# Dynamic convolution and two-way maxout: tap products in one instruction, first chunk ahead of the weights, three of six tap additions moved to an accumulating DMA

## The chip, the cores and the metric

The kernel runs on 1 core of one Trainium2 chip. The metric is the device time of the whole program in microseconds (us). The profile's span is a little shorter (491.3 us; the first three runs of the kernel before have the median 492.15 us). Runs come with a state, fast or slow; unless said otherwise fast runs are compared. A ratio below is the mean time of one kernel's fast runs over the mean of the other's fast runs in the same rounds, so it is not quite the ratio of the medians that are quoted.

## The reference, cut to what matters

For each of 8 x 4160 tokens, the softmax of 7 weights per head (8 heads) mixes the token's own row and the six rows before it; the result goes through a maxout layer:

```python
w = exp(weight_gen - max); w = w / sum(w)           # (B, S, 8, 7)
out = einsum('bshk,bskhg->bshg', w, x_unf)          # 7 taps, 192 channels
h1 = x @ w1;  h2 = x @ w2                           # 192 -> 1024, x is now `out`
y = maximum(h1, h2) @ w_out                         # 1024 -> 192
```

The kernel uses max(h1, h2) = h1 + relu(h2 - h1): it keeps w2 - w1 ("wd") for the hidden layer and folds w1 @ w_out into small matrices ("w10") once at the start.

## The kernel before

Each of the 128 partitions holds 260 token columns. A **chunk** of mostly 16 columns is loaded and convolved at a time; a **unit** of 8 columns is what TensorE takes per pass of the outer loop, so a chunk is mostly two units. At the ends both are smaller: chunks 0 to 2 give units 0 to 3, chunk 3 gives units 4 and 5, and so on. One chunk on VectorE (the `yield` lines and the address patterns are cut):

```python
def conv(ci):                                   # a generator, stepped between units
    sum_t = reduce_sum(e_t); rec_t = reciprocal(sum_t)   # e_t: the exponential, by ScalarE
    en_t = e_t * rec_t
    mul(0, 3)                                   # m_t[k] = x shifted by k * weight k, taps 0..2
    mul(3, 6)
    add(m_t[:, 0:3 * n], 0, 3, 3)               # taps 0..2 += taps 3..5
    mul(6, 7)
    add(m_t[:, 0:n], 0, 1, 1)
    add(m_t[:, 2 * n:3 * n], 2, 6, 1)
    add(y_t, 0, 2, 1)                           # y_t: the chunk's result
```

The outer loop, shortened:

```python
for u in range(NU + 1):
    target = UNITS[min(u + 3, NU - 1)][0]
    while queued <= target and queued < NCH:
        exp(queued)                             # ScalarE
        conv_q.append(queued); queued += 1
        load(loaded); loaded += 1               # GpSimd's DMA queue: weights and x of a later chunk
    if u + 1 < NU:
        conv_flush(UNITS[u + 1][0])             # the chunk that unit u + 1 needs, to its end
        transpose(u + 1)                        # DMA transpose y_t -> yt, from SyncE's queue
    for i in range(4):
        # hidden matmuls of unit u (hdp), ReLU on ScalarE (rd_t), output matmuls of unit u - 1 (op_ps)
        ...
        conv_step(1)
```

Each engine has its own list of instructions, in the order in which they are written here, and in the timelines shown below it works through it in that order: the exponential of chunk 5, at 117.15 us, stands behind the last ReLU of unit 4, at 116.23.

The softmax here doesn't subtract the row's maximum and nothing guards it: scores larger than these inputs give would overflow.

## Time and profile before

| | before |
|---|---|
| time, median | 492.15 us |
| TensorE busy | 426.4 us (87%) |
| VectorE busy | 421.4 us (86%) |
| a two-unit chunk on VectorE / on TensorE | 25.70 / 25.24 us |
| first hidden matmul / first of unit 4 | 47.19 / 102.64 us |
| x load of a big chunk, issue to landing | 8.0 us |
| transpose, issue to landing, median | 5.4 us |

The two engines are nearly balanced, so neither may get slower.

### The profile page before, as it was taken

Reading aid. Unit: us, or ns where it says so; the run is one execution under the profiler, and the core shown is the slowest. Engines: PE = TensorE matmul, PEld = TensorE weight load, DVE = VectorE, ACT = ScalarE, POOL = GpSimd, SP = SyncE. Lnnn points to the kernel's source line nnn. Section 1 sums busy time; section 2 is a strip of 40 time slices with the busy share of each in tenths; the row PEclk is TensorE's granted clock in tenths of the full one; section 3 lists DMA queues with packets and bytes.
Section 4 is the critical chain, followed back from the end, with each engine's and each line's share of the span. In section 5 each row is a group of like instructions: output and inputs, shape, how many; then the busy total and the mean of one; then the engine's idle time right before and its main releaser. Section 6 shows DMA issues by size and latency. Waiting matters only on the chain.

```text
span 491.3 us, 8185 instructions
## 1 busy us (share of the span) xinstructions
PE 426.4 (87%) x3598; PEld 270.3 (55%) x3598; DVE 421.4 (86%) x185; ACT 336.5 (68%) x436; POOL 20.6 (4%) x43
## 2 busy tenths in 40 slices
PE   0041958569999999999999999899999999999997
PEld 0030524336666666665666666566666666666676
DVE  0178999999999999999999999999999999996000
ACT  1142728438787878786787878687878787877774
POOL 2000000000000000000000000000000000000000
PEclk9995979869999999999999999999999999999999
DMA  7726475473929192919383848556474838062312
GB/s 181 242 66 117 87 168 136 77 178 58 261 42 267 33 242 64 248 65 215 105 213 106 176 145 138 182 126 195 96 224 78 232 58 209 1 192 66 114 66 97
DMA packets 62164, 68.36 MB, mean 139 GB/s; under 512 B 52313, under 2 KB 53593, under 8 KB 60336
## 3 DMA queue, kind: packets, MB, share of 16 engines
q1 hardware_dynamic: 58000, 42.30, 31.3%
q0 software_dynamic: 4128, 25.54, 24.6%
q8 instruction: 28, 0.46, 0.4%
q14 instruction: 8, 0.07, 0.0%
HBM read 47.56 MB, written 25.56 MB: 149 GB/s over the span
## 4 chain that ended last, share of the span: by engine, by line
PE 73%; DVE 13%; DMA 11%; issue 1%; ACT 1%; SPq 0%; POOL 0%; POOLq 0%; DVEq 0%
PE op_ps L310 31%; PE hdp L261 20%; PE hdp L276 12%; DMA yt<-y_t 7%; PE op_ps L297 6%; DVE m_t L140 6%; DVE m_t L149 4%; PE op_ps L305 4%; DMA ws<-in_moe_w_dram 2%; DMA wso<-in_moe_w_out_dram 1%; DVE en_t L128 1%; DVE y_t L149 1%; DMA xb_t<-in_x_dram 1%; DVE sum_t L122 1%; DVE rec_t L125 1%
## 5 line engine op out<-in xcount | busy, mean ns | idle before, releaser
L287 ACT ACTIVATE rd_t<-hdp 128x1024 bf16<-128x1024 f32 (+1 forms) x272 | 267.6, 986 | 115.0 <-PE hdp L276 77.1
L310 PE MATMUL op_ps<-wo,rd_t 128*128 128x192 bf16 x2080 | 215.4, 247 | 0.0
L310 PEld LDWEIGHTS <-rd_t 128*128 128x128 bf16 x2080 | 177.0, 98 | 23.5 <-issue 0.6
L140 DVE TENSOR_TENSOR m_t<-xb_t,en_t 128x9216 bf16<-128x9216 bf16 (+5 forms) x54 | 188.8, 3524 | 0.6
L149 DVE TENSOR_TENSOR m_t<-m_t 128x3072 bf16<-128x3072 bf16 (+5 forms) x54 | 136.8, 2561 | 0.6
L261 PE MATMUL hdp<-yt,wdE 128*128 128x512 bf16 (+1 forms) x272 | 101.9, 375 | 31.6 <-DMA yt<-y_t 30.2
L261 PE MATMUL hdp<-yt,wdO 128*128 128x512 bf16 (+1 forms) x272 | 102.0, 375 | 0.0
L276 PE MATMUL hdp<-yt,wdR 64*128 64x512 bf16 (+1 forms) x544 | 82.1, 378 | 1.0 <-ACT rd_t L287 1.0
L321 ACT COPY o_t<-op_ps 128x384 f32<-128x384 f32 x130 | 61.6, 474 | 2.5 <-PE op_ps L310 2.3
L276 PEld LDWEIGHTS <-wdR 64*128 64x128 bf16 x544 | 16.3, 94 | 58.7 <-issue 58.3
L261 PEld LDWEIGHTS <-wdE 128*128 128x128 bf16 x272 | 26.8, 98 | 34.9 <-DMA yt<-y_t 20.0
L297 PE MATMUL op_ps<-w10R,yt 128*128 128x384 bf16 x130 | 44.0, 339 | 0.0
L297 PEld LDWEIGHTS <-yt 128*128 128x128 bf16 x130 | 12.4, 96 | 53.2 <-issue 52.8
L128 DVE TENSOR_TENSOR en_t<-e_t,rec_t 128x1792 bf16<-128x1792 bf16 (+2 forms) x18 | 33.2, 1845 | 0.6
L305 PEld LDWEIGHTS <-yt 128*128 128x128 bf16 x260 | 25.6, 98 | 14.6 <-issue 0.3
L305 PE MATMUL op_ps<-w10E,yt 128*128 128x192 bf16 x130 | 32.2, 248 | 0.0
L305 PE MATMUL op_ps<-w10O,yt 128*128 128x192 bf16 x130 | 32.1, 247 | 0.0
L149 DVE TENSOR_TENSOR y_t<-m_t 128x3072 bf16<-128x3072 bf16 (+2 forms) x18 | 28.8, 1602 | 0.6
L261 PEld LDWEIGHTS <-wdO 128*128 128x128 bf16 x272 | 26.8, 98 | 2.6 <-issue 2.6
L214 PE MATMUL tp<-ident,w1E 128*128 128x128 bf16 x8 | 2.2, 274 | 25.1 <-ACT w1E L197 16.8
L102 POOL DMA_DIRECT2D xb_t<-in_x_dram x17 | 9.0, 530 | 350.3 <-DVE m_t L140 350.3
L122 DVE TENSOR_REDUCE sum_t<-e_t 128x128 f32<-128x896 bf16 (+2 forms) x18 | 17.8, 989 | 4.4 <-ACT e_t L112 4.4
(30 smaller groups left out, 67.4 us busy)
## 6 DMA issues: line engine op xcount, KB each, us to landing
out_dram<-o_t SPq DMA_DIRECT2D x31, 768.0 KB, 3.5
xb_t<-in_x_dram POOLq DMA_DIRECT2D x14, 1056.0 KB, 8.0
wg_t<-in_weight_gen_dram POOLq DMA_DIRECT2D x14, 448.0 KB, 8.9
ws<-in_moe_w_dram SPq DMA_DIRECT2D x4, 512.0 KB, 8.8
xb_t<-in_x_dram POOLq DMA_DIRECT2D x2, 672.0 KB, 8.6
ws<-in_moe_w_dram SPq DMA_DIRECT2D x4, 256.0 KB, 10.8
xb_t<-in_x_dram POOLq DMA_DIRECT2D x1, 864.0 KB, 7.3
wso<-in_moe_w_out_dram SPq DMA_DIRECT2D x1, 768.0 KB, 6.4
```

Source lines behind the costliest of these rows:

```text
L102: nc.gpsimd.dma_start(out=xb_t, in_=bass.AP(tensor=x.tensor, offset=(c0 - PAD) * D, ap=[[CPP * D, P], [1, (To + PAD) * D]]),)
L122: nc.vector.reduce_sum(out=sum_t, in_=_sub(e_t, 0, [[K, TH], [1, K]]), axis=AX.X)
L128: nc.vector.tensor_tensor(out=_sub(en_t, 0, [[2, TH], [2 * TH, K], [1, 2]]), in0=_sub(e_t, 0, [[K, TH], [1, K], [0, 2]]), in1=_sub(rec_t, ...
L140: nc.vector.tensor_tensor(out=m_t[:, k0 * n:k1 * n], in0=_sub(xb_t, k0 * D, [[D, nk], [1, n]]), in1=_sub(en_t, k0 * TH * 2, [[2 * TH, nk], ...
L149: nc.vector.tensor_tensor(out=dst, in0=m_t[:, a * n:(a + w) * n], in1=m_t[:, b * n:(b + w) * n], op=ALU.add)
L261: nc.tensor.matmul(hd_ts[u, f][:, j * 512:j * 512 + N], lhsT=wd[kind][:, f * P:(f + 1) * P], rhs=_sub(yt_ts[u], 2 * j * P, [[3 * P, n // 2 ...
L276: nc.tensor.matmul(hd_ts[u, f][:, j * 512:j * 512 + N], lhsT=wd["R"][r, f * P:(f + 1) * P], rhs=_sub(yt_ts[u][r, :], P, [[3 * P, n // 2], ...
L287: nc.scalar.activation(out=_sub(rd_ts[u], f * 1024, [[512, 2], [1, N]]), in_=_sub(hd_ts.pop((u, f)), 0, [[512, 2], [1, N]]), func=AF.Relu,)
L297: nc.tensor.matmul(op[:, 0:2 * D], lhsT=yt[:, (3 * i + 1) * P:(3 * i + 2) * P], rhs=w10R, start=True, stop=False, skip_group_check=True,)
L305: nc.tensor.matmul(op[:, sl], lhsT=yt[:, (3 * i + 2 * j) * P:(3 * i + 2 * j + 1) * P], rhs=(w10E, w10O)[j], start=False, stop=False, skip_ ...
L310: nc.tensor.matmul(op[:, sl], lhsT=rd[:, f, j * 512 + i * P:j * 512 + (i + 1) * P], rhs=wo[:, f * D:(f + 1) * D], start=False, stop=(f == ...
L321: nc.scalar.copy(out=o_ts[u][:, 2 * i * D:2 * (i + 1) * D], in_=op_ts.pop((u, i))[:, 0:2 * D])
```

## The change

The intent is to free VectorE. The seven products become one instruction. Three of the six additions (taps 0..2 += taps 3..5) go to a DMA that adds to its destination. As that takes a while, the remaining additions of a chunk (`conv2`) are issued one chunk later, behind the products of the next chunk. Chunk 0 is also loaded and convolved before the weights are prepared, and the weights are loaded only once. The core of the diff, with cuts:

```diff
-        mul(0, 3) ... mul(3, 6) ... add(m_t[:, 0:3 * n], 0, 3, 3) ... mul(6, 7) ... (further adds)
+        nc.vector.tensor_tensor(out=m_t, in0=_sub(xb_t, 0, [[D, K], [1, n]]), in1=..., op=ALU.mult)
+        if ci + 2 < len(CHUNKS):
+            load(ci + 2)
+        m_ts[ci] = m_t
+        nc.gpsimd.dma_start(out=m_t[:, 0:3 * n], in_=m_t[:, 3 * n:6 * n], accum_op=ALU.add,
+                            max_dma_last_dim=4096)
+
+    def conv2(ci):
+        nc.vector.tensor_tensor(out=rows(m_t, 2, 2, 0), in0=rows(m_t, 2, 2, 0),
+                                in1=rows(m_t, 5, 2, 1), op=ALU.add)
+        nc.vector.tensor_tensor(out=y_t, in0=m_t[:, 0:n], in1=m_t[:, 2 * n:3 * n], op=ALU.add)
...
+        exp(0); conv(0); conv2(0)              # ahead of the weight differences
...
     for u in range(NU + 1):
+        while queued < NCH and queued <= UNITS[min(u + 3, NU - 1)][0]:
+            exp(queued)
+            conv(queued)
+            if queued > 1:
+                conv2(queued - 1)
+            queued += 1
         if u + 1 < NU:
-            conv_flush(UNITS[u + 1][0])
             transpose(u + 1)
```

More of the change, by code (lines that the diff above doesn't have):

```diff
@@ L51 @@
         c += 16
-    CHUNKS.append((c, [8, CPP - c - 8] if CPP - c > 8 else [CPP - c]))
+    while c < CPP:
+        CHUNKS.append((c, [min(8, CPP - c)]))
+        c += 8
     assert sum(sum(u) for _, u in CHUNKS) == CPP
@@ L67 @@
     psm = ctx.enter_context(tc.tile_pool(name="psm", bufs=1))
+    pm = ctx.enter_context(tc.tile_pool(name="pm", bufs=2))
     pen = ctx.enter_context(tc.tile_pool(name="pen", bufs=2))
@@ L73 @@
     wg_ts, xb_ts, y_ts, yt_ts = {}, {}, {}, {}
-    e_ts = {}
+    e_ts, m_ts = {}, {}
     zero_t = consts.tile([P, PAD * D], BF16, name="zero_t")
@@ L122, in conv @@
         nc.vector.reduce_sum(out=sum_t, in_=_sub(e_t, 0, [[K, TH], [1, K]]), axis=AX.X)
-        yield
         rec_t = psm.tile([P, TH], FP32, name="rec_t", tag="rec")
@@ L133, in conv, with rows @@
         )
-        yield
         xb_t = xb_ts.pop(ci)
-        m_t = psm.tile([P, K * n], BF16, name="m_t", tag="m")
-        def mul(k0, k1):
-            nk = k1 - k0
-            nc.vector.tensor_tensor(
-                out=m_t[:, k0 * n:k1 * n],
-                in0=_sub(xb_t, k0 * D, [[D, nk], [1, n]]),
-                in1=_sub(en_t, k0 * TH * 2,
-                         [[2 * TH, nk], [2, TH], [0, D // H // 2], [1, 2]]),
-                op=ALU.mult,
-            )
-        def add(dst, a, b, w):
-            nc.vector.tensor_tensor(out=dst, in0=m_t[:, a * n:(a + w) * n],
-                                    in1=m_t[:, b * n:(b + w) * n], op=ALU.add)
-        mul(0, 3)
-        yield
-        mul(3, 6)
-        yield
-        add(m_t[:, 0:3 * n], 0, 3, 3)
-        yield
-        mul(6, 7)
-        add(m_t[:, 0:n], 0, 1, 1)
-        yield
-        add(m_t[:, 2 * n:3 * n], 2, 6, 1)
+        m_t = pm.tile([P, K * n], BF16, name="m_t", tag="m")
+        nc.vector.tensor_tensor(
+            out=m_t,
+            in0=_sub(xb_t, 0, [[D, K], [1, n]]),
+            in1=_sub(en_t, 0, [[2 * TH, K], [2, TH], [0, D // H // 2], [1, 2]]),
+            op=ALU.mult,
+        )
+        if ci + 2 < len(CHUNKS):
[4 more added lines that the diff above has]
+    def conv2(ci):
+        n = sum(CHUNKS[ci][1]) * D
+        m_t = m_ts.pop(ci)
+        def rows(t, step, cnt, at):
+            return _sub(t, at * n, [[step * n, cnt], [1, n]])
+        nc.vector.tensor_tensor(out=rows(m_t, 2, 2, 0), in0=rows(m_t, 2, 2, 0),
+                                in1=rows(m_t, 5, 2, 1), op=ALU.add)
         y_t = py.tile([P, n], BF16, name="y_t", tag="y")
-        add(y_t, 0, 2, 1)
+        nc.vector.tensor_tensor(out=y_t, in0=m_t[:, 0:n], in1=m_t[:, 2 * n:3 * n], op=ALU.add)
         y_ts[ci] = y_t
-        yield
-    N_CONV = 6
+    load(0)
     ident = consts.tile([P, P], BF16, name="ident")
     make_identity(nc, ident)
-    load(0)
+    load(1)
     wd = {k: consts.tile([P, F], BF16, name="wd" + k) for k in "EOR"}
-    w1 = {k: consts.tile([P, F], BF16, name="w1" + k) for k in "ER"}
     wo = consts.tile([P, FCH * D], BF16, name="wo")
@@ L179 @@
     w10R = consts.tile([P, 2 * D], BF16, name="w10R")
-    def rows(kind):
-        return {"E": [(0, 0, P)], "O": [(0, 64, P)], "R": [(0, P, 64), (64, 0, 64)]}[kind]
-    with tc.tile_pool(name="pstage", bufs=2) as pstage, \
+    with tc.tile_pool(name="pstage", bufs=1) as pstage, \
          tc.tile_pool(name="pstage_ps", bufs=2, space=bass.MemoryType.PSUM) as pstage_ps:
-        for kind in "ERO":
-            st = []
+        ws = {}
+        for kind, r0, nr in (("E", 0, P), ("T", P, 64)):
             for wi, wsrc in enumerate((moe_w1, moe_w2)):
-                t = pstage.tile([P, F], FP32, name=f"ws{wi}", tag=f"ws{wi}")
-                for (p0, r0, nr) in rows(kind):
-                    nc.sync.dma_start(
-                        out=t[p0:p0 + nr, :],
-                        in_=bass.AP(tensor=wsrc.tensor, offset=r0 * F, ap=[[F, nr], [1, F]]),
-                    )
-                st.append(t)
-            if kind in w1:
-                nc.scalar.copy(out=w1[kind], in_=st[0])
-            nc.vector.tensor_tensor(out=wd[kind], in0=st[1], in1=st[0], op=ALU.subtract)
-        wso = pstage.tile([P, FCH * D], FP32, name="wso", tag="wso", bufs=1)
+                t = pstage.tile([nr, F], FP32, name=f"ws{wi}{kind}")
+                nc.sync.dma_start(
+                    out=t, in_=bass.AP(tensor=wsrc.tensor, offset=r0 * F, ap=[[F, nr], [1, F]]),
+                )
+                ws[kind, wi] = t
+        wso = pstage.tile([P, FCH * D], FP32, name="wso")
         nc.sync.dma_start(
@@ L203 @@
         )
-        nc.scalar.copy(out=wo, in_=wso)
-        exp(0)
-        for _ in conv(0):
-            pass
-        load(1)
-        w1t = pstage.tile([P, FCH * 2 * P], BF16, name="w1t", tag="w1t", bufs=1)
+        exp(0)
+        conv(0)
+        conv2(0)
+        for kind, dst in (("E", wd["E"]), ("T", wd["R"][0:64, :])):
+            nc.vector.tensor_tensor(out=dst, in0=ws[kind, 1], in1=ws[kind, 0], op=ALU.subtract)
+        nc.sync.dma_start(out=wd["R"][64:P, :], in_=wd["E"][0:64, :])
+        nc.sync.dma_start(out=wd["O"][0:64, :], in_=wd["E"][64:P, :])
+        nc.sync.dma_start(out=wd["O"][64:P, :], in_=wd["R"][0:64, :])
+        w1 = {}
+        for kind, nr in (("E", P), ("T", 64)):
+            w1[kind] = pstage.tile([nr, F], BF16, name="w1" + kind)
+            nc.scalar.copy(out=w1[kind], in_=ws[kind, 0])
+        nc.scalar.copy(out=wo, in_=wso)
+        w1t = pstage.tile([P, FCH * D], BF16, name="w1t")
         for fi in range(FCH):
-            tp = pstage_ps.tile([P, 2 * P], BF16, name="tp", tag="tp")
-            for j, kind in enumerate("ER"):
+            tp = pstage_ps.tile([P, D], BF16, name="tp", tag="tp")
+            for c0, kind, nr in ((0, "E", P), (P, "T", 64)):
                 nc.tensor.matmul(
-                    tp[:, j * P:(j + 1) * P], lhsT=w1[kind][:, fi * P:(fi + 1) * P],
-                    rhs=ident, is_transpose=True, skip_group_check=True,
-                )
-            nc.scalar.copy(out=w1t[:, fi * 2 * P:(fi + 1) * 2 * P], in_=tp)
-        nc.vector.memset(w10R, 0.0)
-        for d0, kind in ((0, "E"), (64, "O"), (P, "R")):
+                    tp[:, c0:c0 + nr], lhsT=w1[kind][:, fi * P:(fi + 1) * P],
+                    rhs=ident[0:nr, 0:nr], is_transpose=True, skip_group_check=True,
+                )
+            nc.scalar.copy(out=w1t[:, fi * D:(fi + 1) * D], in_=tp)
+        nc.gpsimd.memset(w10R, 0.0)
+        for p0, d0, nr, dst in ((0, 0, P, w10E), (0, 64, P, w10O),
+                                (0, P, 64, w10R[0:64, 0:D]), (64, 0, 64, w10R[64:P, D:2 * D])):
             pw = pstage_ps.tile([P, D], FP32, name="pw", tag="pw")
@@ L223 @@
                 nc.tensor.matmul(
-                    pw, lhsT=w1t[:, fi * 2 * P + d0:fi * 2 * P + d0 + P],
+                    pw[p0:p0 + nr, :], lhsT=w1t[:, fi * D + d0:fi * D + d0 + nr],
                     rhs=wo[:, fi * D:(fi + 1) * D],
@@ L227 @@
                 )
-            if kind == "E":
-                nc.scalar.copy(out=w10E, in_=pw)
-            elif kind == "O":
-                nc.scalar.copy(out=w10O, in_=pw)
-            else:
-                nc.scalar.copy(out=w10R[0:64, 0:D], in_=pw[0:64, :])
-                nc.scalar.copy(out=w10R[64:P, D:2 * D], in_=pw[64:P, :])
+            nc.scalar.copy(out=dst, in_=pw[p0:p0 + nr, :])
     prd = ctx.enter_context(tc.tile_pool(name="prd", bufs=2))
@@ L334 @@
     NCH = len(CHUNKS)
-    conv_q = []
-    conv_gen = {}
-    first_unit = [next(u for u in range(NU) if UNITS[u][0] == ci) for ci in range(NCH)]
-    def conv_step(k):
-        while k > 0 and conv_q:
-            ci = conv_q[0]
-            if ci not in conv_gen:
-                conv_gen[ci] = conv(ci)
-            try:
-                next(conv_gen[ci])
-                k -= 1
-            except StopIteration:
-                conv_q.pop(0)
-    def conv_flush(ci):
-        while ci not in y_ts:
-            conv_step(1)
-    transpose(0)
-    exp(1)
-    load(2)
-    conv_q.append(1)
-    conv_flush(1)
-    conv_step(1)
-    loaded, exped, queued = 3, 2, 2
+    queued = 1
     prev_evac = None
     for u in range(NU + 1):
-        target = UNITS[min(u + 3, NU - 1)][0]
-        while queued <= target and queued < NCH:
-            if exped <= queued:
-                exp(queued)
-                exped += 1
-            conv_q.append(queued)
+        while queued < NCH and queued <= UNITS[min(u + 3, NU - 1)][0]:
[3 more added lines that the diff above has]
+                conv2(queued - 1)
             queued += 1
-            if loaded < NCH:
-                load(loaded)
-                loaded += 1
+            if queued == NCH:
+                conv2(NCH - 1)
+        if u == 0:
+            transpose(0)
         if u + 1 < NU:
-            conv_flush(UNITS[u + 1][0])
             transpose(u + 1)
@@ L399 @@
                 prev_evac = (u - 1, q)
-            conv_step(1)
     if prev_evac is not None:
```

## The prediction

> **What bounds the kernel now.** I read the page top down: busy shares, slices, the chain that ended last, then instruction timelines and waits around two unit boundaries. A unit is the block of 8 (at the ends 4) token columns that TensorE handles in one pass of the outer loop. A chunk is what VectorE and one load handle, mostly two units.
>
> ```profile
> PE 426.4 (87%) x3598; PEld 270.3 (55%) x3598; DVE 421.4 (86%) x185; ACT 336.5 (68%) x436; POOL 20.6 (4%) x43
> ...
> PE   0041958569999999999999999899999999999997
> ...
> DVE  0178999999999999999999999999999999996000
> ...
> PE 73%; DVE 13%; DMA 11%; issue 1%; ACT 1%; SPq 0%; POOL 0%; POOLq 0%; DVEq 0%
> ```
>
> Two engines are nearly full. From slice 9 both rows are at 9, so this is a balance, not one bottleneck. The chain stays mostly on TensorE; its VectorE share sits in the first 97 us. Measured in the timeline: the result tiles (y_t) of successive big chunks end every 25.70 us (120.83, 146.52, 172.22), so VectorE's period is 25.70 us. Undisturbed, the first output matmul of a quarter unit recurs every 3.155 us, so a unit takes 12.62 us of TensorE and a two-unit chunk 25.24. VectorE is the slower by 0.46 us a chunk. After 102.64 the excess over the 3.155 us spacing adds up to only about 5 us. Relieving VectorE can therefore save 5 us there; the rest of the gain must come before 102.64.
>
> Three lines show how ScalarE ties VectorE to TensorE, in the timeline:
>
> ```profile
> 116.23 1.02 ACT L287 ACTIVATE rd_t<-hdp 128x1024 bf16<-128x1024 f32 x1 [0.26 <-PE hdp L261]
> 117.15 0.94 ACT L112 ACTIVATE e_t<-wg_t 128x896 bf16<-128x896 f32 x1
> ...
> 122.50 1.08 DVE L122 TENSOR_REDUCE sum_t<-e_t 128x128 f32<-128x896 bf16 x1
> ```
>
> The first is the last ReLU of unit 4, the second the exponential of chunk 5, which begins only when that ReLU is through. Its reader is the sum of chunk 5 at 122.50, when VectorE has finished chunk 4. It was ready 4.4 us early, so this tie costs nothing today.
>
> Three more show what a late y_t costs:
>
> ```profile
> 95.13 1.76 DVE L149 TENSOR_TENSOR y_t<-m_t 128x3072 bf16<-128x3072 bf16 x1
> 96.96 5.10 SPq L245 DMA_TRANSPOSE yt<-y_t  x2
> 102.64 0.61 PE L261 MATMUL hdp<-yt,wdE 128*128 128x512 bf16 x1 [9.45 <-DMA yt<-y_t]
> ```
>
> From the end of y_t (96.89) to the first matmul of its unit it is 5.75 us.
>
> **What the Trainium skill says.** "VectorE: DVE Perf Modes", section "The perf-mode tier table", gives bf16 tensor_tensor twice the base rate, 1224 ns for 2048 elements. The trace agrees: 9216 elements took 4955 ns and 3072 took 1751, hence 0.5215 ns an element plus 149 ns.
>
> "TensorE: Matmul & The Clock Gate", Part 1, says that an idle TensorE drops to half rate and recovers after about 3.4 us of work. The trace agrees; in the stretches around the stall of 9.45 us the granted clock (next to last but two) reads
>
> ```profile
> 100.00:105.00 5.00, 2.36 (x8) 0.52 (x9) 4.96 (x2) 0.68 (x1) 0.00 (x0) 0.50 1.04 185
> 105.00:110.00 5.00, 5.00 (x43) 3.56 (x42) 5.00 (x2) 3.21 (x6) 0.00 (x0) 0.91 0.41 161
> 110.00:115.00 5.00, 5.00 (x44) 2.94 (x42) 4.97 (x2) 3.78 (x5) 0.00 (x0) 1.00 0.00 0
> ```
>
> The unit that began at 102.64 lasted until about 116.77 (the next first output matmul, 117.83, less the usual 1.06), 14.13 us, so such a restart costs 1.5 us.
>
> "DMA: Bandwidth & Descriptors", section "SWDGE vs HWDGE vs iDMA", allows accumulation only from GpSimd's queue; so the additions share a queue with the x loads. "Collectives: The Full Stack", section "The bandwidth ceiling", says that an adding transfer reads two sources and so runs at half of about 31 GB/s per engine. The kernel before has none to compare.
>
> **The change part by part.**
>
> *VectorE per big chunk.* Before: three products (4955 + 4955 + 1752), additions 4958 + 2 x 1751, last addition 1758, and the softmax part, together 25.70 us. After, by the fit: one product of 21504 elements, 11.36; one addition over 6144, 3.35; the last, 1.76; the softmax part 4.16 (sum start to product start, 96.81 to 100.97). Sum 20.6 with gaps, 5 us less. VectorE's instructions are no longer the limit.
>
> *The accumulating DMA.* Source and destination of 3 x 3072 bf16 on 128 partitions are 2.36 MB each. Estimated from the Collectives page: 2.36 MB / (16 x 15.5 GB/s) = 9.5 us, behind an x load of 8.0 us (median to landing). DMA is busy 0.58 of the stretch 103 to 460, 14.9 us a chunk; with this 24.4.
>
> *The start.* The weights shrink from 3 to 1.5 MB and two row blocks come by copies. Chunk 0's product no longer waits for the weights: exponential at about 4.5, product at about 9.2 (its x lands as before, a little earlier), ending at 15. The accumulation follows the x load of chunk 2 and lands about 27; y_t at 30; weight differences 2.5; first hidden matmul at about 38 instead of 47.19. Then VectorE: products of chunks 1 and 2 until 49, a wait of about 5 for the accumulation, y_t of chunk 1 at 57, chunk 3's product until 73, y_t of chunk 2 at 75.6, chunk 4's product (its exponential comes after unit 2, about 76.5) until 93, y_t of chunk 3 at 98. Unit 4 starts at 98 + 5.75, about 104, against 102.64: the early start is eaten, because chunk 3's result now stands behind chunk 4's product.
>
> *The steady loop, which decides.* In the built order of the changed kernel, as of the one before, the exponential of chunk c+2 stands on ScalarE directly after the last ReLU of chunk c's first unit. On VectorE the final additions of chunk c+1 stand behind the product of chunk c+2, and the transpose of chunk c+1 waits for them. Before, that result stood ahead of chunk c+2's softmax. So now a closed loop exists, from a second unit's start to the next unit's start:
> - exponential begins 0.38 after it (117.15 against 116.77) and takes 0.94: 1.32
> - sum, reciprocal, weights: 4.16 plus 0.05 semaphore gap, to 5.53
> - product 11.36, to 16.9
> - two additions and gaps, 5.2, to 22.1
> - transpose and first matmul 5.75, to 27.8
>
> The unit that runs beside it takes 12.62, so TensorE stalls 15.2 us. Then comes the next first unit, restarting slow, 14.13. Period: 27.8 + 14.1 = 41.9 us instead of 25.70. Nothing in this loop is a full engine: VectorE works 20.6 of 41.9.
>
> Sum: unit 4 at 104; twelve periods bring unit 28 to 607. The chunk then pulled in has 8 columns: product 5.76 instead of 11.36, softmax 2.4 instead of 4.16, exponential 0.57 instead of 0.94, 7.8 less; unit 30 at 641. In the kernel before unit 30 started near 436.4 (first output matmul 437.50 less 1.06) and the end came 54.9 later; plus 1.5 for the slow restart: span 697. Time exceeds span by 0.85 (492.15 against 491.3): 698.
>
> **The rivals.**
> - *The loop is open and TensorE is the bound.* For it: VectorE falls to 20.6 against 25.24. Then 104 + (491.3 - 102.64 - 5), about 488. Against it: it needs the exponential ahead of the unit before, and the built order has it behind.
> - *DMA becomes the bound.* For it: 24.4 of 25.24 us, and slices where DMA is at 9 already. With an accumulation at 14 us the period is 29, some 540. Against it: the loop of 41.9 leaves it 17 us of slack, so it shows only if the loop is not there.
> - *A slow accumulation enters the loop.* The products of chunk c+1 end 41.9 us before its additions; load 8 plus accumulation would have to exceed that, four times my estimate. Then above 720.
> - *The early start wins 9 us.* It is hidden: unit 4 waits for chunk 4's product anyway.
>
> **Range and chances.** The loop's terms are measured ones but for the product's fit. Transposes took 3.6 to 7.2 us to land (median 5.3); all drifting by 1.5 us moves 13 periods by 20. The start is sure to 10. Hence 698, from 672 to 722. Slower by over 2% 0.97, within 2% 0.02, faster 0.01: only a misread order would undo 200 us.
>
> **What would show it.** Right: TensorE stalls of about 15 us at every second unit, put down to the transpose; busy rows near 6 for PE and 5 for VectorE; each product preceded by an idle VectorE ended by the exponential; first hidden matmul near 38, unit 4 near 104, product about 11.4 us. Wrong: the additions waiting on the accumulating DMA, DMA at 9 throughout, a steady TensorE, or exponentials that run during the preceding unit.

## More of the kernel before

The prediction shows most lines; three more, from the profile's list of DMA issues of the kernel before, are needed for comparison. The columns are what is moved, the issuing queue, the count, KB each, and the median us from issue to landing (a transpose's size is not given):

```profile
out_dram<-o_t SPq DMA_DIRECT2D x31, 768.0 KB, 3.5
xb_t<-in_x_dram POOLq DMA_DIRECT2D x14, 1056.0 KB, 8.0
...
yt<-y_t SPq DMA_TRANSPOSE x34, 5.4
```

## The result, and the profile after

The changed kernel takes 875.75 us (875.28 to 875.90, 4 runs) against 491.86 us: ratio 1.781, 95% interval 1.777 to 1.784. The prediction had said 698 us, at most 722. So the direction was right and the size was not: 384 us were lost where 206 had been expected.

The head, slices and chain of the page after, the counterparts of the lines in the prediction:

```profile
PE 462.3 (53%) x3606; PEld 284.1 (32%) x3606; DVE 337.4 (39%) x117; ACT 337.2 (39%) x437; POOL 50.4 (6%) x65
...
PE   0545349157092570925709257092570916619698
...
DVE  3566803608136081260712608136081360804500
...
DMA  9698891561925719257192571925619156090832
...
DMA 35%; PE 29%; issue 18%; DVE 16%; ACT 1%; POOL 0%; SPq 0%; DVEq 0%; POOLq 0%
```

No engine is near full. TensorE, VectorE and DMA take turns, in a pattern that repeats every 54.5 us, and DMA leads the chain that ended last. The waits, longest in total (who waited, for whom, us in total, times, longest):

```profile
DVE sum_t L125 <- ACT e_t L115: 453.3, 15, 34.3
PE hdp L250 <- DMA yt<-y_t: 385.9, 17, 27.4
...
DVE m_t L157 <- DMA m_t<-m_t: 29.8, 4, 13.3
```

VectorE waits for the exponential and TensorE for the transpose: the loop that the prediction describes. The additions waited for the accumulating DMA only four times. One round in the timeline after:

```profile
309.06 0.94 ACT L115 ACTIVATE e_t<-wg_t 128x896 bf16<-128x896 f32 x1
310.03 1.08 DVE L125 TENSOR_REDUCE sum_t<-e_t 128x128 f32<-128x896 bf16 x1 [33.90 <-ACT e_t L115]
...
314.20 11.36 DVE L138 TENSOR_TENSOR m_t<-xb_t,en_t 128x21504 bf16<-128x21504 bf16 x1
...
326.38 1.51 POOL L147 DMA_DIRECT2D m_t<-m_t  x1
328.86 1.76 DVE L160 TENSOR_TENSOR y_t<-m_t 128x3072 bf16<-128x3072 bf16 x1
330.68 9.75 SPq L234 DMA_TRANSPOSE yt<-y_t  x1
...
348.90 0.61 PE L250 MATMUL hdp<-yt,wdE 128*128 128x512 bf16 x1 [27.44 <-DMA yt<-y_t]
```

From the exponential's start to the end of y_t (330.62) it is 21.56 us; the prediction's terms give 21.7 for that. But from there to the first matmul it is 18.28 us, where 5.75 had been taken. In this stretch the DMA engines hold the x load and the accumulation, both issued at the end of the product (the list of DMA issues after):

```profile
m_t<-m_t POOLq DMA_DIRECT2D x14, 2304.0 KB, 21.0
...
xb_t<-in_x_dram POOLq DMA_DIRECT2D x14, 1056.0 KB, 9.2
...
yt<-y_t SPq DMA_TRANSPOSE x34, 16.1
```

The accumulation was issued at 326.38 and took 21 us, to about 347.4; the transpose, issued 4 us later, was through 1.5 us after that. Of its 18.3 us, SyncE's instruction that issues it took 9.75; in experiment 2, where no accumulation runs, that instruction took 1.44 us (at 328.30). So part of the delay falls already in the issuing. Four-microsecond stretches of the same time (start:end, length, busy time of PE, PEld, DVE, ACT and POOL with counts, then PEclk, DMA share and GB/s):

```profile
334.00:338.00 4.00, 0.00 (x0) 0.00 (x0) 0.00 (x0) 0.00 (x0) 0.00 (x0) 0.50 1.05 199
338.00:342.00 4.00, 0.00 (x0) 0.00 (x0) 0.00 (x0) 0.00 (x0) 0.00 (x0) 0.50 1.09 206
```

All compute engines stand still while the DMA engines are full (shares a little above 1 come out of the records as they are; read them as full).

### The profile page after: what moved, and what is told of

Its sections match the earlier page's. It is cut to its first block, busy times and chain, and to the rows that moved or that the text cites. A ratio compares the mean times of both kernels' runs of the same rounds, so it can differ in the third digit from the quotient of the medians.

```text
span 874.1 us, 8158 instructions
## 1 busy us (share of the span) xinstructions
PE 462.3 (53%) x3606; PEld 284.1 (32%) x3606; DVE 337.4 (39%) x117; ACT 337.2 (39%) x437; POOL 50.4 (6%) x65
## 3 DMA queue, kind: packets, MB, share of 16 engines
q0 software_dynamic: 17152, 64.18, 38.9%
## 4 chain that ended last, share of the span: by engine, by line
DMA 35%; PE 29%; issue 18%; DVE 16%; ACT 1%; POOL 0%; SPq 0%; DVEq 0%; POOLq 0%
DMA yt<-y_t 31%; PE op_ps L299 11%; PE hdp L250 9%; DVE m_t L157 5%; PE hdp L265 5%; DMA m_t<-m_t 3%; DVE en_t L130 3%; DVE y_t L160 3%; PE op_ps L286 3%; DVE sum_t L125 2%; PE op_ps L294 1%; DVE rec_t L127 1%; DVE m_t L138 1%; ACT e_t L115 1%; DMA xb_t<-zero_t 1%
## 5 line engine op out<-in xcount | busy, mean ns | idle before, releaser
L250 PE MATMUL hdp<-yt,wdE 128*128 128x512 bf16 (+1 forms) x272 | 109.0, 401 | 386.5 <-DMA yt<-y_t 385.9
L299 PE MATMUL op_ps<-wo,rd_t 128*128 128x192 bf16 x2080 | 226.6, 255 | 0.0
L299 PEld LDWEIGHTS <-rd_t 128*128 128x128 bf16 x2080 | 186.7, 102 | 28.0 <-issue 6.4
L138 DVE TENSOR_TENSOR m_t<-xb_t,en_t 128x21504 bf16<-128x21504 bf16 (+2 forms) x19 | 185.0, 9737 | 5.4 <-DMA xb_t<-zero_t 4.8
L250 PE MATMUL hdp<-yt,wdO 128*128 128x512 bf16 (+1 forms) x272 | 109.0, 401 | 0.0
L265 PE MATMUL hdp<-yt,wdR 64*128 64x512 bf16 (+1 forms) x544 | 88.2, 403 | 0.8 <-ACT rd_t L276 0.7
L157 DVE TENSOR_TENSOR m_t<-m_t 128x6144 bf16<-128x6144 bf16 (+2 forms) x19 | 54.9, 2889 | 29.8 <-DMA m_t<-m_t 29.8
L286 PE MATMUL op_ps<-w10R,yt 128*128 128x384 bf16 x130 | 46.3, 356 | 0.0
L85 POOL DMA_DIRECT2D wg_t<-in_weight_gen_dram x19 | 12.2, 643 | 465.3 <-ACT e_t L115 464.4
L294 PEld LDWEIGHTS <-yt 128*128 128x128 bf16 x260 | 26.6, 102 | 16.8 <-issue 4.1
L147 POOL DMA_DIRECT2D m_t<-m_t x19 | 27.6, 1455 | 51.6 <-DVE m_t L138 50.5
```

What stands on the lines that cost most here:

```text
L138: nc.vector.tensor_tensor(out=m_t, in0=_sub(xb_t, 0, [[D, K], [1, n]]), in1=_sub(en_t, 0, [[2 * TH, K], [2, TH], [0, D // H // 2], [1, 2]] ...
L157: nc.vector.tensor_tensor(out=rows(m_t, 2, 2, 0), in0=rows(m_t, 2, 2, 0), in1=rows(m_t, 5, 2, 1), op=ALU.add)
L250: nc.tensor.matmul(hd_ts[u, f][:, j * 512:j * 512 + N], lhsT=wd[kind][:, f * P:(f + 1) * P], rhs=_sub(yt_ts[u], 2 * j * P, [[3 * P, n // 2 ...
L265: nc.tensor.matmul(hd_ts[u, f][:, j * 512:j * 512 + N], lhsT=wd["R"][r, f * P:(f + 1) * P], rhs=_sub(yt_ts[u][r, :], P, [[3 * P, n // 2], ...
L286: nc.tensor.matmul(op[:, 0:2 * D], lhsT=yt[:, (3 * i + 1) * P:(3 * i + 2) * P], rhs=w10R, start=True, stop=False, skip_group_check=True,)
L294: nc.tensor.matmul(op[:, sl], lhsT=yt[:, (3 * i + 2 * j) * P:(3 * i + 2 * j + 1) * P], rhs=(w10E, w10O)[j], start=False, stop=False, skip_ ...
```

## The experiments

My theory after reading the result: the closed loop is what the prediction said, and the one term that was wrong is the transpose, which shares the DMA engines with the accumulation. The rivals: the loop is not the cause; the accumulation does not matter to the transpose; or something else in the new order does it. "Period" is the time from one chunk to the next in the steady part, taken from the stalls of TensorE at unit 4 and unit 28, twelve periods apart (after: 129.05 and 782.60, so 54.5 us). "Transpose" is from the end of y_t to the first matmul of its unit in one round, 18.3 us after.

**1. The accumulation is issued after the transposes (loop kept).**

```diff
-        nc.gpsimd.dma_start(out=m_t[:, 0:3 * n], ..., accum_op=ALU.add, ...)   # directly behind the load
+        pend.append(ci)                         # for the two-unit chunks
...
             transpose(u + 1)
+            if due:                             # one unit later: GpSimd reads yt, then accumulates
+                nc.gpsimd.tensor_copy(out=scr, in_=yt_ts[u + 1][:, 0:2])
+                accumulate(pend.pop(0))
```

> The closed loop stays as in the changed kernel, but GpSimd issues the accumulation of each two-unit chunk only after both transposes of the chunk before it have landed (a tiny GpSimd copy reads their result). My theory: the predicted loop was right and only its transpose term (5.75 us predicted, 18.2 measured) was mis-sized, because the accumulating DMA shares the 16 engines with the transpose. Then the transpose falls to 5.5 to 7.5 us, the period from 54.5 to 42-44 us and the time to 700-735 us. Rival (the x load or the stores slow the transpose, the accumulation does not matter): period stays near 54 and time above 840 us.

Measured 702.6 us (ratio 1.429). The same pair of lines in its timeline:

```profile
318.07 1.76 DVE L175 TENSOR_TENSOR y_t<-m_t 128x3072 bf16<-128x3072 bf16 x1
...
325.06 0.61 PE L265 MATMUL hdp<-yt,wdE 128*128 128x512 bf16 x1 [14.38 <-DMA yt<-y_t]
```

The transpose takes 5.2 us (319.83 to 325.06) beside the x load alone, and the period is 40.9 us (unit 4 at 118.79, unit 28 at 610.04), where the prediction had 41.9. The accumulation is still there, does as much work and only no longer meets the transpose. That settles the term: 173 us of the 178 that the prediction missed come back. That the total comes so near to 698 is partly luck: unit 4 is 14.8 us later than predicted, and twelve periods are together 11.5 us shorter.

**2. The three additions on VectorE, still one chunk behind (loop kept, no accumulation).**

```diff
-        nc.gpsimd.dma_start(out=m_t[:, 0:3 * n], ..., accum_op=ALU.add, ...)
     def conv2(ci):
+        nc.vector.tensor_tensor(out=m_t[:, 0:3 * n], in0=m_t[:, 0:3 * n],
+                                in1=m_t[:, 3 * n:6 * n], op=ALU.add)
```

> No accumulating DMA: the three additions run on VectorE ahead of the other final additions, still behind the product of the next chunk, so the loop is still closed. My theory: the loop gets 4.96 us longer by the addition and 12 us shorter by a transpose of 5.5 to 7 us: period about 47 us, time 745 to 775 us, faster than the changed kernel although VectorE does more. Rival (accumulation harmless for the transpose): period 59, time above 900 us.

Measured 746.45 us (ratio 1.518), period 45.4 us, transpose 3.8 us. Although VectorE works 5 us more per chunk inside the loop, the kernel is 129 us faster than the changed one. The loop by itself, without any accumulating DMA, still costs 254 us against the kernel before: it comes from the order of the instructions (experiment 4 has the same additions with the loop opened).

**3 and 12. The exponential one chunk ahead (loop opened, accumulation as in the change).**

The edit, shortened:

```diff
-            exp(queued)
+            if exped == queued: exp(queued); exped += 1
             conv(queued)
+            if exped < NCH: exp(exped); exped += 1
```

> The accumulation stays as it is; only the exponential of each chunk is put on ScalarE one chunk earlier, which opens the loop. My theory: the stalls of 27 us at every second unit go, VectorE no longer waits for the exponential, and the period falls to what TensorE (25.2) or the DMA engines (26 to 30) allow: 500 to 580 us. Rival (the accumulation and the transposes are by themselves what takes 54 us a chunk, the loop is not the cause): above 800 us.

Two runs, 567.4 us (fast) and 583.1 us (slow), with the profile in the slow one. It was run again:

> The kernel of the third experiment again, because one of its two runs was slow by over 1.5% and the profile fell into that one. If its steady part is bound by the DMA engines: a fast run of 563 to 572 us, DMA at 9 in nearly all slices from the fourth on, and 28 us a chunk. Rival (the waits at its start alone make it slow): the steady part at 25.2 to 25.7 us a chunk.

Measured 579.7 us (576.8 to 581.5; ratio 1.179), outside the range that I had given from a single fast run. Over both experiments, on two chips, this kernel took 567 to 583 us, so the figure is good to some 3% only. The steady part is now at about 28.4 us a chunk (stalls at 213.56 and 469.26, nine chunks apart), and TensorE is nearly full again. Its stretches (columns as above):

```profile
250.00:300.00 50.00, 45.19 (x372) 28.40 (x370) 34.58 (x10) 34.49 (x43) 3.16 (x4) 0.97 1.08 220
300.00:350.00 50.00, 45.48 (x373) 28.31 (x372) 32.32 (x13) 34.67 (x44) 5.20 (x6) 0.93 1.06 216
```

One move of one ScalarE instruction takes off nearly 300 us, so the loop is the larger cause. But the DMA share stands above 1 in these stretches. Share times period gives the DMA time of a chunk: 1.07 x 28.4 = 30.4 us here (1.07 over 213.56 to 469.26), 0.54 x 54.5 = 29.4 us in the changed kernel, 0.58 x 25.7 = 14.9 us in the kernel before. It is the same work, now packed without gaps, and more than the 25.70 us that VectorE needed before. How this reaches TensorE is seen in the chain that ended last, which alternates between one unit and one transpose:

```profile
310.53 10.29 SPq L234 DMA_TRANSPOSE yt<-y_t  x1
...
328.30 0.61 PE L250 MATMUL hdp<-yt,wdE 128*128 128x512 bf16 x1 [4.52 <-DMA yt<-y_t]
```

The result (y_t) was ready at 306.36, but the transpose begins only at 310.53: there are three yt buffers, and TensorE's last read of the one that it needs ends at 310.50. From there to the first matmul of its unit it is 13.3 to 17.7 us in the rounds from 200 to 420 us, where the unit that runs beside it takes 12.62. So by this chain the period is again set by a transpose beside the accumulation. Whether it was this late start or the full DMA engines as such was not separated; by either reading the accumulation does not pay with the exponential ahead. (Its first 160 us also hold stalls of 31 and 23 us at units 4 and 6, for transposes that meet accumulations; they are part of the 580.)

**4. Exponential ahead, and the three additions on VectorE.** Experiments 2 and 3 together.

> The open loop of the third experiment, but with the three additions on VectorE and no accumulating DMA. Against that run it shows what the accumulation costs where the loop is not closed. My theory: 28.2 us a chunk there is the DMA engines' limit, so here the period falls to 25.2 to 25.7 and unit 4 comes near 98 to 103: 480 to 500 us. Rival (something else in the new order holds the period at 28): 540 to 570 us.

Measured 491.8 us (ratio 1.000, interval 0.995 to 1.005), unit 4 at 103.37. Against 12 this shows the price of the accumulation with an open loop: some 88 us. The loop without the accumulation costs 254 us (experiment 2); the two add up to 342 of the 384 us, so roughly the last 40 us come from their meeting. Against the kernel before it shows that the delay by one chunk eats the early start, as the prediction had argued: unit 4 comes no earlier than 102.64.

**6. The accumulation ahead of the x load in GpSimd's queue.**

```diff
-        if ci + 2 < len(CHUNKS): load(ci + 2)
         m_ts[ci] = m_t
         nc.gpsimd.dma_start(out=m_t[:, 0:3 * n], ..., accum_op=ALU.add, ...)
+        if ci + 2 < len(CHUNKS): load(ci + 2)
```

> GpSimd issues the accumulation first and the x load two chunks ahead second; everything else as in the changed kernel. It shows how long the accumulation takes when no load is ahead of it in its queue. My theory: about 12 to 14 us to landing at chunks of 16 columns (21.0 with the load ahead), and the transpose, which is issued some 4 us later, ends about when the accumulation does: 9 to 13 us instead of 18, period 45 to 50, time 770 to 830 us. Rival (any traffic of that queue slows the transpose alike): transpose 17 to 19, time 860 to 885 us.

Measured 897.3 us (ratio 1.825), period 56.1 us: my theory missed. The accumulation lands after 17.0 us, but the transpose is not over with it:

```profile
332.80 1.76 DVE L160 TENSOR_TENSOR y_t<-m_t 128x3072 bf16<-128x3072 bf16 x1
...
354.43 0.61 PE L250 MATMUL hdp<-yt,wdE 128*128 128x512 bf16 x1 [29.02 <-DMA yt<-y_t]
```

It takes 19.9 us and ends with the load that follows the accumulation (issued at 331.21, median landing 22.2 us, so about 353.4). In this order, too, the transpose ends within some 1.5 us of the moment at which the other queue has run dry. This suggests that the transpose has to outlast the whole batch in that queue, whatever stands last in it; the next experiment shows a transpose that does not.

**7. The accumulation in pieces of 1024 bytes.**

```diff
-                            max_dma_last_dim=4096)
+                            max_dma_last_dim=1024)
```

> The changed kernel with one edit: the accumulation is cut into pieces of 1024 bytes instead of 3072, three times as many. Theory of turns: the engines serve the two queues packet by packet in turn, a transpose is about 100 small packets on each engine, and it is slow because it gets only one turn per large packet of the other queue; with three times as many packets there it gets its turns sooner: transpose 18 falls to 10 to 14 us, time to 780 to 840 us, if the accumulation itself does not slow. Rival (shared bandwidth, no matter in what pieces, or pieces joined into the same packets): transpose 17 to 19 us, time 865 to 890 us.

Measured 865.1 us (ratio 1.759): transpose 16.8 us, period 53.2. The pieces were indeed three times as many (42240 packets in that queue instead of 17152, the loads included in both), and the accumulation got slower, 25.4 us to landing. The transpose now ends before it (at 344.69 against about 349), which speaks a little for turns by packet, but the gain of 1.5 us is not the 4 to 8 that this theory asked for. How the engines divide themselves between the two queues stays open.

**10. The same bytes as a plain copy.**

```diff
-        nc.gpsimd.dma_start(out=..., in_=..., accum_op=ALU.add, max_dma_last_dim=4096)
+        nc.gpsimd.dma_start(out=..., in_=..., max_dma_last_dim=4096)
```

> The changed kernel with the addition taken out of the DMA: the same bytes in the same pieces and queue as a plain copy, so the result is wrong on purpose. It shows whether the accumulating itself or merely the bytes in the queue cost the time. My theory: an accumulation reads two sources, a copy one, so the transfer takes about half (6 to 8 us instead of 13 behind the load, landing 14 to 16 us after issue instead of 21.0), the transpose 10 to 13 us instead of 18, period 46 to 49 us, time 760 to 815 us. Rival (the addition is free, bytes and pieces decide): landing 20 to 22 us and time 865 to 880 us.

Measured 778.0 us (ratio 1.581), period 47.5 us, transpose 11.9 us. From the list of DMA issues:

```profile
m_t<-m_t POOLq DMA_DIRECT2D x14, 2304.0 KB, 14.5
...
xb_t<-in_x_dram POOLq DMA_DIRECT2D x14, 1056.0 KB, 9.1
```

The copy lands 6.5 us earlier than the accumulation (14.5 against 21.0), and the transpose is 6.4 us shorter. The addition has a price of its own, and the transpose pays it one for one.

**11. The remaining additions ahead of the next chunk's product (no delay by a chunk, accumulation kept).**

```diff
+            if queued > 1: conv2(queued - 1)
             exp(queued)
             conv(queued)
-            if queued > 1: conv2(queued - 1)
```

> The changed kernel with the final additions of the chunk before put ahead of the exponential and product of the next chunk on VectorE, that is, without the one-chunk delay. The loop through the exponential is open, but VectorE must now wait for the accumulation in each chunk. My theory: VectorE's cycle becomes softmax and product 15.5, accumulation landing 21 after the product, additions 5.1, together about 42 us a chunk; the transpose follows when the queue is empty and is short: 680 to 730 us. Rival (only the loop through the exponential matters): 480 to 580 us.

Measured 738.3 us (ratio 1.500), a little above my range; the period is 42.0 us as I had worked out, the start was later (unit 4 at 136.99). Each chunk waits for the accumulation:

```profile
296.64 3.36 DVE L157 TENSOR_TENSOR m_t<-m_t 128x6144 bf16<-128x6144 bf16 x1 [21.61 <-DMA m_t<-m_t]
```

Here no transpose is in flight beside it, and it still lands 20.6 us after its issue (median). The load ahead of it lands 9.4 us after its own issue, which comes 0.5 us before, so the accumulation itself takes 20.6 - 8.9 = 11.7 us. This is an upper figure: a load of 448 KB is issued 3.1 us behind it in the same queue (321.17 against 318.05 in the next round) and lands about when it does.

**5, 8 and 9. What is worth keeping.** Experiment 8 is the kernel before with the products in one instruction (`mul(0, 7)`) and nothing else.

> The kernel before with the seven tap products of a chunk in one instruction and nothing else: what this part of the change is worth alone. Two instruction overheads of 149 ns less per chunk: VectorE's period 25.40 instead of 25.70 us, unit 4 about 1.2 us earlier and up to 4 us of small stalls gone: 486 to 491 us. Rival (x buffer is freed at another time, loads and transposes meet otherwise): 492 or more.

Measured 490.3 us; ratio 0.997, interval 0.993 to 1.001, so no difference is shown. VectorE's period is 25.68 us against 25.70 (y_t starts at 220.91 and 246.59): from the start of the products to the start of y_t it is 19.85 us against 19.86, since several of the separate instructions began 0.08 us before the one ahead of them had ended, so that there was hardly an overhead left to save.

Experiment 5 is the changed kernel with all additions on VectorE directly behind the product of their own chunk: no accumulation, no delay, early start kept.

```diff
-        nc.gpsimd.dma_start(out=m_t[:, 0:3 * n], ..., accum_op=ALU.add, ...)
+        conv_adds(ci)            # taps 0..2 += 3..5, then the additions of conv2, in the same chunk
...
-            if queued > 1: conv2(queued - 1)
```

> The changed kernel without the accumulating DMA and without the one-chunk delay: one product instruction, first chunk ahead of the weights, all six additions on VectorE directly behind the product of their own chunk. The loop from exponential to transpose then closes over four units instead of two (27 + 6 us of latency against 37.9 us), so it should not bind. My theory: first hidden matmul near 31 us, unit 4 near 84 instead of 102.6, then TensorE at 25.2 us a chunk: 462 to 480 us, faster than both kernels. Rival (the early start is hidden, as my prediction said of the whole change): 485 to 492 us.

Measured 478.3 us (ratio 0.972, interval 0.967 to 0.976), unit 4 at 88.57 instead of 102.64. Its timeline shows an idle VectorE at the start:

```profile
23.91 1.21 DVE L194 TENSOR_TENSOR wdR<-ws1T,ws0T 64x1024 bf16<-64x1024 f32 x1
32.17 0.62 DVE L125 TENSOR_REDUCE sum_t<-e_t 128x64 f32<-128x448 bf16 x1 [7.05 <-ACT e_t L115]
```

Chunk 1's exponential stood on ScalarE behind all weight preparation. Experiment 9 moves it up:

```diff
         exp(0)
+        exp(1)
         conv(0)
```

> The fifth experiment with one move: the exponential of chunk 1 stands on ScalarE ahead of the weight casts, so that VectorE does not sit idle for the 7.05 us that it did there before chunk 1's sum. My theory: VectorE is the bound in that kernel from its start on (25.6 us a chunk), so all of it moves up: unit 4 near 82 instead of 88.6, and 469 to 474 us. Rival (the time is set elsewhere, by TensorE or the weights): 476 to 480 us.

Measured 471.2 us (470.98 to 471.98, 6 runs) against 491.8: ratio 0.958, interval 0.955 to 0.961; unit 4 at 81.45. The 7 us arrive in full. This version beats both kernels, by the early start; it also keeps the single product instruction, which alone showed no difference (experiment 8), and the changed kernel's order of loads, which was not tried alone.

## Why the prediction was right or wrong

- **The closed loop: right.** Exponential, softmax part, product (11.36 us, as the fit had it) and additions took 21.56 us, 21.7 by the prediction. Experiments 3, 4 and 12 open the loop by moving one instruction and its stalls of 27 us in every chunk go; experiment 2 keeps it without any accumulation, and it still costs 254 us.
- **"transpose and first matmul 5.75": wrong, and nearly the whole error.** It measured 18.3 us. The term had been read from a transpose that met an x load of 8 us only; in the changed kernel it meets a load and, behind it, an accumulation that had been issued 4 us before. Experiment 1 removes just this meeting: the transpose takes 5.2 us and the time is 702.6 us, inside the predicted range of 672 to 722 (with two smaller misses that cancel, as said there).
- **The sum, with the measured terms.** Period 54.5 instead of 41.9: twelve of them make 151 us. Unit 4 came at 129.05 instead of 104, 25 us, where the prediction had called the start sure to 10: the first hidden matmul was nearly right (39.78, predicted 38), but on the way the transposes of chunks 1, 2 and 3 took 13.2, 21.9 and 17.6 us instead of 5.75 each, part of it beside other work. From unit 28 to 30 it was 35.2 us (34.1 predicted), from there to the end 56.3 (56.4). 151 + 25 + 1 is the 177 us between the predicted span of 697 and the measured 874.1. A slip of 1 us stands in the step from span to time: 0.85 was taken from a span and a median of different runs; the profiled run took 493.06 us for the span of 491.3, so 1.8.
- **The accumulation's own size: somewhat too small.** Estimated 9.5 us, by its landing at most 11.7 (experiment 11). By the DMA time of a whole chunk (predicted as 24.4 us, measured as 29.4, against 14.9 in the kernel before) it is some 14.5; the two ways of measuring are not reconciled.
- **"DMA becomes the bound": dismissed for the wrong reason.** I argued that a loop of 41.9 us leaves the DMA engines 17 us of slack. On average it does (their share after was 0.50 to 0.55 in the steady rounds). But the work comes at one moment, the end of the product, and the transpose follows 4 to 5 us later. An average says nothing about what lies in the queues when a critical transfer starts. Once the loop was open, the DMA engines were full and the period was 28.4 us (experiment 12); the prediction had 29 for this case, with an accumulation of 14 us.
- **"A slow accumulation enters the loop": did not happen in this way.** I had looked only for additions that wait for the accumulation. They waited 29.8 us in all. It entered through the transpose, and none of my rivals named that.
- **"The early start wins 9 us ... is hidden": right for the delayed order** (experiment 4: unit 4 at 103.4, 491.8 us), and it shows where the gain lies: without the delay it is worth 14 us, and 21 us with chunk 1's exponential moved up.
- **The restart of TensorE** was put at 14.13 us for the first unit. After: the next exponential starts at 363.95, which by the same 0.38 puts the second unit's start at 363.57, 14.67 us after 348.90. This is a small error.
- **The range** came from transposes in the old company (3.6 to 7.2 us), with 1.5 us as the drift of them all. It did not allow for new traffic in the same place, though the change adds just that.

Left open: how the engines share themselves between the transpose and the other queue (experiments 6 and 7), and how much of the delay arises in the issuing by SyncE. Not run: an accumulation kept out of the transpose's way, as in experiment 1, with the exponential ahead, and more than three yt buffers.

## What to carry to other kernels

When a change reorders instructions on in-order engines, write down the cycle of waits that leads back to itself and add up its latency; such a cycle can set the time although no engine is more than 53% busy. Take the duration of a transfer on that cycle from a moment with the same traffic, not from the old kernel: ask which other DMA the change starts just before it. An addition on an idle DMA queue is not free if a latency-critical transfer shares the engines; here the additions on VectorE were the better choice in two pairs (2 against the change, 4 against 12). In the closed loop an accumulation kept out of the transpose's way was better than they were (experiment 1, 702.6 us, against experiment 2, 746.5 us), but still far slower than the kernel before.

## What the Trainium skill lacked or had wrong

- "DMA: Bandwidth & Descriptors", section "Queues, rings and completion order", tells that the engines take turns between queues by packets, but gives nothing from which the delay of a DMA transpose beside other traffic could be estimated. The runs show 3.8 us with the engines otherwise idle, 5.2 to 5.75 us beside an x load of 1056 KB, 11.9 us with a copy of 2304 KB behind that load, 18.3 us with an accumulation in the copy's place, and 16.8 us with that accumulation in pieces of a third.
- No page gives the rate of an accumulating DMA within SBUF. The estimate from "Collectives: The Full Stack", section "The bandwidth ceiling", was 9.5 us for 2.36 MB; the runs show 11.7 us at most by its landing, and some 14.5 us by the DMA time of a chunk. That an addition reads two sources and so runs at half of a copy's rate fits: the plain copy landed 14.5 us after its issue and the load ahead of it 8.6 us after the same moment (9.1 less 0.5), which leaves 5.9 us for the copy. By the DMA time of a chunk (0.47 x 47.8 = 22.5 us with the copy, less the 14.9 of the kernel before) it is 7.6 against 14.5.
